# Converting eight instead of sixteen stages' weights ahead of the first block, with a new order of work, in a fused attention and two-layer network kernel

## The chip, the core and the metric

The kernel runs on one core of a Trainium2 chip. The core has a matrix engine (TensorE, PE in the profile, with its weight loads shown as PEld), a vector engine (VectorE, DVE), an activation engine (ScalarE, ACT), a general engine (GpSimd, POOL) and a queue for transfers (SyncE, SP). ACT can issue transfers too; all transfers run on the same sixteen DMA engines. The metric is device time in microseconds (us) of one run of the whole program.

## What is computed

The reference chains three parts. B = 2 batches, H = 8 heads, S = 768 positions, D = 64.

```python
q_assign = np.argmax(np.einsum('bhsd,hcd->bhsc', q_n, c_n), axis=-1)   # 16 centroids per head
k_assign = np.argmax(np.einsum('bhsd,hcd->bhsc', k_n, c_n), axis=-1)
mask = q_assign[:, :, :, None] == k_assign[:, :, None, :]
scores = np.where(mask, scale * np.matmul(q, k.transpose(0, 1, 3, 2)), -1e9)
attn = softmax(scores); x = np.matmul(attn, v)          # 1536 tokens x 512

h = x @ w_in                                            # 512 x 2048
g = np.where(h >= 1, h, np.where(h <= -1, 0.0, (h + 1) ** 2 / 4))
x = g @ w_out                                           # 2048 x 512

h = (x @ w1) * (x @ w2) @ w3                            # 512 x 1024, 1024 x 1024
out = h @ w_out2                                        # 1024 x 512
```

All five weight matrices come as 64-bit floats.

## The kernel before

**Blocks and stages.** A block is one batch of 768 tokens. Attention of a block is cut into units of two heads (a *pair*, 0 to 3 in block 0) and these into tiles of 128 queries by 768 keys, 48 tiles a block, numbered 0 to 95. For each tile PE makes the scores (`s`, L859), DVE their row maximum (`smax`, L867), GpSimd scales it (`sbias`, L872), ACT takes the exponential (`sexp`, L880), and PE transposes the result (`spT`, L897), which ACT or DVE copies out (`sT`, L352 or L354); in block 1 most tiles are split in two 16-bit halves and transposed by a DMA instead. When six tiles are there, PE multiplies them with v (`pv`, L968 and L976). Before the scores of block 0 stand the centroid products (`am`, L539, which need k or q of two pairs), some ten DVE instructions of the form L555 to L590 that turn them into masks, and small triangular matmuls (`ah`, L580).

Behind attention, block 0 passes through *stages* of the two networks, in the order of a list `seq`: `h` and `y` stages for the first (16 of each, L1239), then 16 `ab` stages and 8 `o` stages. Each stage needs a weight chunk of 128 x 512. The product of w3 and w_out2 (`wp`, L1169) is made beside the attention of block 0. Block 1 goes through the same stages later, most of them by a scheme with seven products instead of eight (L1492).

**A weight chunk** is made in `chunk`. A chunk that still has 64-bit words is loaded (512 KB, L1101, issued by ACT), converted to 32 bits by two ACT instructions (`wabs` L1107, `wr` L1111) and two DVE instructions (`wc`, L1115 and L1121), and, if it is used again, stored as 256 KB into the DRAM tensor `wd` (SP, L1126). For use it is split into a high half (`whi`, ACT or DVE) and a low half (`wlo`, GpSimd or DVE, L357), since PE makes three passes over split operands. A chunk that lies in `wd` already is only loaded (256 KB, L1103, by ACT) and split. The first stages of `seq` are converted ahead, beside the attention of block 0, one between every few steps of `wp`:

```python
ahead = [weights_of(st) for st in seq[:AHEAD]]
ahead_n = {n for n, _ in ahead}
...
while ahead and len(ahead) * 2 * KF2 > AHEAD * (2 * KF2 - 1 - n):
    x, src = ahead.pop(0)
    chunk(t + dt / 2, src, True, False, keep=x)
...
return chunk(t, wd[n], False, needs=[("wd", n)]) if blk or n in ahead_n else chunk(t, src, True, keep=n)
```

With `AHEAD = 16` these are the stages h 0 to 5, y (0, 0 to 3), h 6 to 9 and y (1, 0 to 1); all later ones are converted in the stage itself ("in place").

**The order.** Nothing schedules at run time. A table of characters, `ORDER`, lists all 3036 steps of the kernel and for each the engine that does it where there is a choice; the steps are emitted in this order, so each engine has its instructions in the order in which they stand there. Waits between engines are set where one step reads or overwrites what another made. Transfers share eight completion semaphores in turn, so a transfer that takes one up again waits until the transfer that had it before has landed. PE also has 40 filler steps (`idle_mm`, L469, two matmuls each as the profile counts them) that multiply an identity and feed nothing; score tile 6 comes behind all of them.

**The first loads.** SP loads k and q of the four pairs of block 0 (`kq0`, L513, 384 KB each, eight loads) and then v of pair 0 (L736). ACT issues the first four chunks of w_out2 (L1101, shown as in_w_out_dram) and the first of w3. ACT's first work is to round q and k to the format of PE (`qh`, `kh`, `k2h`, `q1h`, all L352; `qh1.0` is the rounding of q of pair 1, head 0), DVE's and GpSimd's to make the remainders (`qlo`, `klo`, L357).

Of the kernel before, what the change touches and what calls it, by code (L numbers as in the profile page):

```python
# [43 lines left out]
    ",4,(,*,,,6<6<F<J&9<L<N<8<:<<&E&I<?+m+|,#,.&K,8,:,<<s,%<V,0,2,><g&>%%<@,@,L=*=:<e,B,D+g,N,P,F,R,X,Z,],_<i<k<Z"
    "<n<]<p,e,g<`<a;|<0<2,H,T,a,J<u+i+l,u,w=J<w=X<y<|+o=#%@&@&B<B<Q<R,V,c,y,|=,=<=i=>-(&P=.-#-*+r-,-.-4-6-%-8-:=0"
    "<q=%&c-0-2=@+s=2=4=6=B=D=(%>=y=N-<-@&U-B-D=L=Z=]-L,i,l=P=R=U=V&L-X-Z-]-N-P>0=_,m,o-F->=k>@=a=m=o=d=e=q=s>#-_"
    "=|>P-R-H-u-K-w-y>%>(>4>2>6-e-g=8=F,r-a.(.*.,>D-T-V&_-c&i>a-|>8,s=g=u>+&l&o&e&[=H>-.4.6.8=w>:&W&^&R&b&n>B>F>H"
    ".#-i-m>K&X>L&u..>o.%.0-k.@.B.3.D-o?#>.>=>>%*>e&s.L.N>R>T>V>c&g?4.:.X.<.Z>N>q>s-q.F>X>Z%B.P.R.T.>?(>g>u?%.]?F"
    "._>i.H.J.V>w?*>l>z>]?,?.?0>n>~.a.u.c?V/(/4/*/,&z&|/@-s.w/B/D(&?8?i?@&w>_?2?B?D/.(-($%,/6?6&q?J?H((%D.m.y.|/#"
    "?:?L(.?Z?X?]?<?N/8/:/<?>/%?_?k?m?o?a?Q?q?R/0/2/>%.%0%2.e.g?y%4?s?u/F%F/L/N%H%6/H%J?T?c?e@2@B/J/X%L%8@T@#/P/R"  # L50
    "/T@,?g%:%</Z.i.k?|@4@e0(0*@%.o@(@*/]/_/e/g/V.q?w@.@0/a/c.s@w@6/u/w(*@D0,0.@8@:@=/y@>%N040608@F@H@J@X/|/m@i@V"
    "@g@Z00%P0#0%%R@k@m@]@`@a@N@L@o%T@@@PA.0:020<0?0@0L0N0P0B0D@y@|/i/k/oA2A#A%A)A*0X@q@RA:@c@s@u0u0w0y0FA@0R0T/q"
    "0Z0]APAcA0A40H0J0W0|0_A,A<A>0e0gABADAF(0(2/sA6A8(4(61#0a0c1(1*0iAs1416ATARAVAX0lAZAH1,1.AeAgAiA]AkAKAM1%181:"
    "AwB%0m0o1012AmAo1X1Z1@1L1N1P1B1D1](:Au(=ANA_AaB,1<1R1T(8(AAy(>(BA|(MB#(N1_1FAqB(1H1>B*(D1e1g1J1V(FBJ(H1a1d0r"
    "1i2*(Z(J0s2,2.1u1k1w1y20B.B022(P1|(R24Bi1m1o1rC.BLBO1s2#2%26(TBkBmB2B4B6CL2((V(X282:2<B8B>B@Ck2>BBC12F2H2J2@"
    "2B2DBPBR2LBTBDB;2NB=BV2PBFBIB]B_BaBcBfC2C4C6FLC82T2V2XCNFe2c2eBXCQ2gC:Bg2RBZ2Z2^2_BoBqC<BsB|C#2i2kC?D0BuBxC&"
    "C(2m2a2oC@CBCD3%3(C+(]3*BzCRCTCn3,CoCWCFCH3436383/D>30D3C_CaCcCeC,CX3:3<D#3>2q323B2y3@CK(b3D(d(_(e3P3RCZD@D4"
    "D6D%DLD(3F3HD*3K3L3NCg(h3T3VDZ3XC^3ZD:CjD9CqCsCuCwDB2s3_D<3a3cDN3m3]D]3oCz(iDi3q3e3hDDDG3i3k(tD-E.3sG#(lDHDJ"
    "DPDR2u(nD_4>Da3u3wDk2w2|DTEL(pDn(uC~3#3y4042FP44463|Dc4@4B)(DVE1E2(w4D4GDeDg(q484:4H4JEkD/DYF0ENF>EP(yDoDqDs"
    "4L4N4<4PFiDuDxFND|E#4RFR4#EnFTEoE%E(4TGL4VDz4XFg4ZE4E6E*Fk4]4_E-FmFoE8E:4%4(E@EBF24aG(4*4,Gu4.FVF54c4e4gEEEF"  # L60
    "G%E<E?EI(|)#)%)*G*G,G.F#5:F%F(F*ERETEWEXEKHDE_5<5>F@F6F8FBEaE[E]GPEcEe5@Gy4i4k4m5B5D5FGNGRGT4oEqFYFZEsEuEwF:"
    "4q4s4uF-4w4y4|FqFsEyHmGwG|FHH#F<5H5JHHF/I,EhFJHFEjHJHLGVH%HNFDFFHq5#5,5.5LG05%5(FaFc5*G3E~F]FyF|HoHsHu5N5PHw"
    "F_FuGXGZH)IDI05V5X5R5T5ZH+I.FwI2I4I]G@GBGDGF5]5e5g5i5_5aGHGJ),G4G6).G9)1I65cIa)2G]G_5kHQGa5mHR)4G:G<5s50545u"
# [1694 lines left out]
```

## Time and profile before

| | us |
|---|---|
| median of 3 runs | 719.14 (718.37 to 720.06) |
| the profiled execution, its own time | 719.4 |
| its span, first to last instruction | 717.7 |
| PE / DVE / ACT / POOL busy | 697.5 / 615.3 / 467.4 / 279.6 |

The span is what the profile divides up; 1.7 us of the profiled execution's time lie around it. Matmuls are pipelined, so busy time of PE does not mean that PE is at its peak, but time in which PE is not busy is a wait of the whole chain when nothing else is left for PE to do. TensorE's granted clock is 0.998 of full speed over the span.

### The profile page before, as it was taken

To read this page: it belongs to the slowest core of one execution; us is meant where nothing else is said; L and a number is where in the kernel's file an instruction comes from. 1 tells how busy PE (TensorE), PEld (TensorE's weight loads), DVE (VectorE), ACT (ScalarE), POOL (GpSimd) and SP (SyncE) were. 2 spreads that over 40 slices of the span, in tenths; PEclk is the share of its full clock that TensorE was granted. 3 is DMA by queue.
4 is the path that set the end of the run, shared out by engine and by line. 5 is a ranking of instruction groups with operands and counts; after the bars stand their busy time and mean duration, and the time that the engine had idled before them with its cause. 6 is when DMAs were issued, how large, how long until landed. Compare 5 with 4: busy or idle time off the path is not lost.

```text
span 717.7 us, 12011 instructions
## 1 busy us (share of the span) xinstructions
PE 697.5 (97%) x4185; PEld 633.1 (88%) x4185; DVE 615.3 (86%) x1087; ACT 467.4 (65%) x873; POOL 279.6 (39%) x351
## 2 busy tenths in 40 slices
PE   4999999999999999999999999999999999999998
PEld 1967777677798989899989999999999999999997
DVE  6989999999989989999989998668888797999940
ACT  7889999878876677896786756324844444543211
POOL 2343424222334324344443332323644525387520
PEclk9999999999999999999999999999999999999999
DMA  8247866977989989798889987663133112122211
GB/s 323 85 147 232 296 212 217 293 246 232 229 187 194 227 204 228 193 222 222 232 213 239 227 224 186 136 196 120 45 103 88 46 59 73 59 61 74 87 63 56
DMA packets 122509, 121.58 MB, mean 169 GB/s; under 512 B 80656, under 2 KB 89296, under 8 KB 122448
## 3 DMA queue, kind: packets, MB, share of 16 engines
q1 hardware_dynamic: 99888, 61.39, 34.7%
q10 hardware_dynamic: 22560, 59.42, 26.6%
q8 instruction: 33, 0.54, 0.3%
q14 instruction: 28, 0.23, 0.1%
HBM read 75.79 MB, written 22.28 MB: 137 GB/s over the span
## 4 chain that ended last, share of the span: by engine, by line
PE 80%; ACT 5%; DVE 5%; issue 2%; DMA 1%; ACTq 0%; POOL 0%; SPq 0%; DVEq 0%; POOLq 0%
PE mo L1239 37%; PE sc L1492 9%; PE sc L859 7%; PE mo L1492 6%; PE sc L1239 5%; PE av L976 3%; PE mo L1169 3%; PE av L1239 3%; PE sc L897 2%; PE av L968 2%; PE av L1492 2%; ACT P L880 2%; DVE nm L867 1%; ACT pt L352 1%; DMA wf<-wp 1%
## 5 line engine op out<-in xcount | busy, mean ns | idle before, releaser
L1239 PE MATMUL mo<-X,whl 128*128 128x384 f32 x912 | 169.0, 338 | 0.8 <-DVE Yp L354 0.8
L1239 PEld LDWEIGHTS mo<-X,whl 128*128 128x128 f32 x912 | 158.5, 188 | 3.1 <-DVE Yp L354 1.2
L357 POOL TENSOR_TENSOR whl<-wf,whl 128x512 fp32r<-128x512 f32 x69 | 92.0, 1335 | 128.4 <-DVE whl L354 53.6
L1239 PE MATMUL mo<-G,whl 128*128 128x384 f32 x684 | 126.2, 339 | 0.0
L1239 PEld LDWEIGHTS mo<-G,whl 128*128 128x128 f32 x684 | 120.4, 188 | 0.8 <-ACT phl L352 0.3
L867 DVE TENSOR_REDUCE nm<-sc 128x1 f32<-128x768 f32 x96 | 89.7, 950 | 9.5 <-PE sc L859 6.9
L872 POOL TENSOR_SCALAR nm<-nm 128x1 f32<-128x1 f32 x96 | 30.1, 313 | 132.8 <-DVE nm L867 122.4
L352 ACT ACTIVATE whl<-wf 128x512 fp32r<-128x512 f32 x63 | 39.3, 628 | 36.8 <-PE mo L1239 19.0
L859 PE MATMUL sc<-k,q 128*128 128x512 f32 (+1 forms) x192 | 53.5, 359 | 1.9 <-ACT pt L352 1.2
L1107 ACT ACTIVATE wf<-w 128x512 f32<-128x512 f32 x72 | 48.0, 674 | 11.3 <-POOL whl L357 6.3
L1111 ACT ACTIVATE w<-w,down 128x512 uint32<-128x512 uint32 x72 | 54.6, 767 | 0.2
L880 ACT ACTIVATE P<-sc,nm 128x768 f32<-128x768 f32 x52 | 46.6, 900 | 11.3 <-POOL nm L872 6.6
L1121 DVE SCALAR_TENSOR_TENSOR wf<-w,wf 128x512 uint32<-128x512 uint32 x72 | 51.8, 726 | 1.2
L1115 DVE SCALAR_TENSOR_TENSOR wf<-wf,w 128x512 uint32<-128x512 uint32 x72 | 49.6, 695 | 1.0 <-ACT wf L1107 0.4
L859 PE MATMUL sc<-kq 80*128 80x512 f32 (+1 forms) x192 | 49.4, 339 | 0.0
L880 ACT ACTIVATE sc<-sc,nm 128x768 f32<-128x768 f32 x44 | 38.2, 869 | 15.9 <-POOL nm L872 15.4
L357 DVE TENSOR_TENSOR phl<-sc,phl 128x768 f16<-128x768 f32 x44 | 41.8, 951 | 6.6 <-ACT phl L352 5.9
L897 PEld LDWEIGHTS sc<-ident,P 128*128 128x128 f32 x312 | 35.0, 140 | 10.4 <-ACT P L880 6.8
L897 PE MATMUL sc<-ident,P 128*128 128x128 f32 x312 | 40.7, 275 | 2.4 <-ACT P L880 2.3
L352 ACT ACTIVATE pt<-sc 128x768 f32<-128x768 f32 (+1 forms) x46 | 36.4, 811 | 5.8 <-PE sc L897 4.7
L859 PEld LDWEIGHTS sc<-k,q 128*128 128x128 f32 x192 | 31.5, 189 | 9.0 <-ACT pt L352 3.7
L357 DVE TENSOR_TENSOR whl<-wf,whl 128x512 fp32r<-128x512 f32 x43 | 31.0, 721 | 9.2 <-ACT whl L352 8.7
(238 smaller groups left out, 1458.8 us busy)
## 6 DMA issues: line engine op xcount, KB each, us to landing
wf<-wd ACTq DMA_DIRECT2D x64, 256.0 KB, 2.7
w<-in_w_out_dram ACTq DMA_DIRECT2D x24, 512.0 KB, 4.6
wd<-wf SPq DMA_DIRECT2D x48, 256.0 KB, 3.4
w<-in_w3T_dram ACTq DMA_DIRECT2D x16, 512.0 KB, 4.6
...
```

The lines of the kernel that those rows point to most:

```text
L352: nc.scalar.activation(out=out, in_=in_, func=AF.Copy)
L357: (nc.gpsimd if e == "POOL" else nc.vector).tensor_tensor(out=out, in0=a, in1=b, op=ALU.subtract)
L859: nc.tensor.matmul(ps[:, n], q[0:n_rows, q0:q0 + 128], k[0:n_rows, n], start=first, stop=not first)
L867: nc.vector.tensor_reduce(out=nm, in_=T[("sc", b), s], axis=AX.X, op=ALU.max, negate=True)
L880: nc.scalar.activation(out=new(("P", b), s).rearrange("p n s -> p (n s)") if by_pe(s) else T[("sc", b), s], in_=T[("sc", b), s], func=AF.E ...
L897: nc.tensor.transpose(T[("sc", b), s][:, c], p[:, c], ident)
L1107: nc.scalar.activation(out=T["wf", i], in_=T[w64, i].bitcast(F32)[:, :, 1], func=AF.Abs, scale=float(2.0 ** -112))
L1111: nc.scalar.activation(out=lo, in_=lo, func=AF.Identity, scale=float(2.0 ** -29 - 2.0 ** -41), bias=down)
L1115: nc.vector.scalar_tensor_tensor(out=w, in0=w, scalar=3, in1=T[w64, i][:, :, 0], op0=ALU.logical_shift_left, op1=ALU.bitwise_or)
L1121: nc.vector.scalar_tensor_tensor(out=w, in0=T[w64, i][:, :, 1], scalar=0x80000000, in1=w, op0=ALU.bitwise_and, op1=ALU.bitwise_or)
L1239: nc.tensor.matmul(acc, w[:, a, k4 * 128:(k4 + 1) * 128], rhs(c, k4), start=(first and k4 == 0 and n == 0), stop=(last and k4 == 3 and n = ...
L1492: nc.tensor.matmul(ps, lhs(av, a, k), rhs(bv, c, k), start=k == 0 and n == 0, stop=k == 1 and n == 2,)
```

## The change

`AHEAD` becomes 8. The stages h 0 to 5 and y (0, 0 to 1) are still converted ahead; y (0, 2 to 3), h 6 to 9 and y (1, 0 to 1) are now converted in place. For each of these eight a load of 64-bit words and the four conversion steps move into its stage, the store into `wd` (for block 1) with them, and the load from `wd` in block 0 falls away: 3028 steps instead of 3036. `ORDER` is replaced by another table for these steps, so that also steps that have nothing to do with weights stand elsewhere or on another engine.

```diff
@@ -36,63 +36,63 @@
 ORDER = (
-    "###%#*#,#0#.$.$V%X#(%V%[#2$0#4%e%h%c%q$6$8$:$<$>$X$_$a$c$e%b%k$2$4$H%]:m:|%y&,%_%i;0;>$@$B$D%m;L$]$Z$q#B$g$i"
+    "###%#:#<#*#,#0#.#($0$V%X%[$.#2#4$Z$]$X$4%e%h%]%V%b%c%q%y&,$6$8$:$<%|#8#Z%_:m:|$_$a%m%k;0$q#N$>$@$c$e$D$2$H$s"
...
 )
@@ -372,7 +372,7 @@
     LATE = 8.0
     W_AFTER = []
     V_AHEAD = 4
-    AHEAD = 16
+    AHEAD = 8
     U_DVE = 4
     N_IDLE, N_IDLE1 = 40, 0
     W_SIDE = 1
```

**SP at the start.** These are the first loads of k and q (in_kT_dram, in_qT_dram) and of v in SP's queue, before:

```order
L513 DMA kq_119<-in_kT_dram 128x768
L513 DMA kq_119<-in_qT_dram 128x768
L513 DMA kq_119<-in_kT_dram 128x768
L513 DMA kq_119<-in_qT_dram 128x768
L513 DMA kq_119<-in_kT_dram 128x768 x2
L513 DMA kq_119<-in_qT_dram 128x768 x2
L736 DMA raw_93<-in_vT_dram 128x768
```

And with the change:

```order
L513 DMA kq_119<-in_kT_dram 128x768
L513 DMA kq_119<-in_qT_dram 128x768
L513 DMA kq_119<-in_kT_dram 128x768
L513 DMA kq_119<-in_qT_dram 128x768 x3
L513 DMA kq_119<-in_kT_dram 128x768 x2
L736 DMA raw_93<-in_vT_dram 128x768
```

The pairs, which the rows do not name, were k0 q0 k1 q1 k2 k3 q3 q2 and are now k1 q0 k0 q2 q3 q1 k3 k2: the last load was q of pair 2 and is now k of pair 2.

**ACT at the start.** These are ACT's rounding of k and q (L352; kq_105 and kq_106 belong to pair 0, k_101, kq_107 and q_104 to head 0 of pair 1) and its first weight loads (L1101, w), before:

```order
L352 ACTIVATE kq_105<-kq_119 64x768
L352 ACTIVATE k_99<-kq_119 64x768
L352 ACTIVATE kq_106<-kq_119 64x768
L352 ACTIVATE k_100<-kq_119 64x768
L352 ACTIVATE kq_106<-kq_119 64x768
L352 ACTIVATE kq_105<-kq_119 64x768
L1101 DMA w_113<-in_w_out_dram 128x1024
L1101 DMA w_114<-in_w_out_dram 128x1024
L352 ACTIVATE k_101<-kq_119 64x768
L352 ACTIVATE q_102<-kq_119 64x768
L352 ACTIVATE kq_106<-kq_119 64x768
L1101 DMA w_115<-in_w_out_dram 128x1024
```

And with the change:

```order
L352 ACTIVATE kq_105<-kq_119 64x768
L352 ACTIVATE kq_106<-kq_119 64x768
L352 ACTIVATE kq_105<-kq_119 64x768
L352 ACTIVATE k_99<-kq_119 64x768
L352 ACTIVATE k_100<-kq_119 64x768
L352 ACTIVATE k_101<-kq_119 64x768
L352 ACTIVATE kq_107<-kq_119 64x768
L352 ACTIVATE q_102<-kq_119 64x768
L1101 DMA w_113<-in_w_out_dram 128x1024
L1101 DMA w_114<-in_w_out_dram 128x1024
L352 ACTIVATE q_103<-kq_119 64x768
L352 ACTIVATE kq_106<-kq_119 64x768
```

The first weight load now stands behind the rounding of k and q of pair 1 (k_101, kq_107); before it stood behind that of pair 0 alone.

**ACT in the first stages of block 0's network.** These rows stand beside the first y stages (Yp is their sum) and the attention tiles of block 1 (sc, phl, L880); wf<-wd is the load of a chunk that was converted ahead. Before:

```order
L352 ACTIVATE k_100<-raw_94 64x768
L1103 DMA wf<-wd 128x512
L880 ACTIVATE sc_1912,su<-sc_1912,nm 128x768
L1103 DMA wf<-wd 128x512
L880 ACTIVATE sc_1913,su<-sc_1913,nm 128x768
L1101 DMA w_115<-in_w_in_dram 128x1024
L352 ACTIVATE Yp<-mo_1907 128x384
L352 ACTIVATE phl_112<-sc_1913 128x768
L352 ACTIVATE whl<-wf 128x512
```

And with the change, beside the h stages just ahead of them:

```order
L880 ACTIVATE sc_1865,su<-sc_1865,nm 128x768
L1101 DMA w_113<-in_w_in_dram 128x1024
L1111 ACTIVATE w_114<-w_114,down 128x512
L1107 ACTIVATE wf<-w_114 128x512
L880 ACTIVATE sc_1866,su<-sc_1866,nm 128x768
L352 ACTIVATE phl_111<-sc_1866 128x768
L352 ACTIVATE phl_112<-sc_1865 128x768
L352 ACTIVATE whl<-wf 128x512
L1111 ACTIVATE w_115<-w_115,down 128x512
```

The 256 KB loads from wd have gone; 512 KB loads of 64-bit words and the two conversion steps L1111 and L1107 stand there.

## Rows read from the trace of the kernel before

**Rows 1.** The page, busy time and share of the span by engine.
```profile
PE 697.5 (97%) x4185; PEld 633.1 (88%) x4185; DVE 615.3 (86%) x1087; ACT 467.4 (65%) x873; POOL 279.6 (39%) x351
```

**Rows 2.** Windows by stage, whole span: each engine's busy us, PE clock, DMA share.
```profile
core 0: us, PE busy (x) PEld busy (x) DVE busy (x) ACT busy (x) POOL busy (x), PEclk, DMA share, GB/s
0.00:18.00 18.00, 7.45 (x37) 1.98 (x38) 10.99 (x29) 13.69 (x19) 5.31 (x14) 1.00 0.89 323
18.00:38.00 20.00, 19.91 (x141) 18.71 (x140) 18.18 (x29) 17.16 (x29) 6.27 (x9) 0.91 0.31 102
38.00:100.00 62.00, 60.68 (x368) 45.65 (x367) 57.59 (x96) 57.15 (x102) 25.41 (x34) 1.00 0.68 219
100.00:160.00 60.00, 57.83 (x348) 40.69 (x347) 57.29 (x87) 52.49 (x89) 19.63 (x25) 1.00 0.77 249
160.00:250.00 90.00, 88.84 (x537) 77.25 (x536) 81.76 (x130) 68.68 (x127) 29.07 (x44) 1.00 0.89 215
250.00:300.00 50.00, 48.52 (x293) 45.52 (x292) 45.27 (x75) 37.04 (x67) 16.80 (x23) 1.00 0.85 207
300.00:450.00 150.00, 150.00 (x951) 141.06 (x950) 138.01 (x221) 109.33 (x198) 58.32 (x70) 1.00 0.90 220
450.00:717.70 267.70, 264.25 (x1524) 262.26 (x1522) 206.26 (x425) 111.88 (x248) 118.75 (x135) 1.00 0.28 84
```

**Rows 3.** Timeline of PE to 22 us: start, us, operation, [idle before, releaser].
```profile
16.82 0.85 PE L539 MATMUL sc<-kq,cT 128*32 128x384 f32 x8 [2.52 <-DMA kq<-in_qT_dram]
```

**Rows 4.** Timeline of ACT to 22 us, its weight loads: issue time and us to issue.
```profile
5.54 0.39 ACTq L1101 DMA_DIRECT2D w<-in_w_out_dram  x1
...
8.13 0.35 ACTq L1101 DMA_DIRECT2D w<-in_w_out_dram  x1
...
10.08 0.33 ACTq L1101 DMA_DIRECT2D w<-in_w_out_dram  x1
```

**Rows 5.** Windows as in rows 2, of single stretches.
```profile
0.00:24.10 24.10, 13.55 (x74) 7.98 (x75) 16.14 (x38) 17.81 (x25) 7.12 (x15) 0.93 0.71 258
6.00:8.00 2.00, 0.33 (x2) 0.18 (x2) 1.32 (x4) 1.99 (x4) 0.00 (x0) 1.00 0.90 283
10.00:12.00 2.00, 1.65 (x9) 0.55 (x10) 1.90 (x4) 1.98 (x3) 1.42 (x2) 1.00 1.04 421
400.00:420.00 20.00, 20.00 (x130) 18.77 (x127) 18.53 (x30) 11.37 (x22) 6.90 (x9) 1.00 1.00 239
```

**Rows 6.** Timeline of DVE, 18 to 25 us, first and last row.
```profile
18.30 0.58 DVE L555 STREAM_TRANSPOSE P<-sc 128x384 f32<-128x384 f32 x1 [2.09 <-PE sc L580]
...
24.14 0.96 DVE L867 TENSOR_REDUCE nm<-sc 128x1 f32<-128x768 f32 x1 [0.54 <-PE sc L859]
```

**Rows 7.** Timeline of PE, 40 to 42 us: the first product with v.
```profile
41.16 1.19 PE L968 MATMUL av<-pt,vn 128*64 128x384 f32 x6
```

**Rows 8.** Waits of PE: us in total, times, longest.
```profile
PE sc L897 <- ACT P L880: 2.3, 4, 1.1
...
PE sc L859 <- ACT pt L352: 1.2, 5, 0.3
```

**Rows 9.** Groups by line: busy us, mean ns of one | idle before.
```profile
L357 POOL TENSOR_TENSOR whl<-wf,whl 128x512 fp32r<-128x512 f32 x69 | 92.0, 1335 | 128.4 <-DVE whl L354 53.6 <-ACT whl L352 47.6 <-issue 17.4
...
L1111 ACT ACTIVATE w<-w,down 128x512 uint32<-128x512 uint32 x72 | 54.6, 767 | 0.2
...
L1121 DVE SCALAR_TENSOR_TENSOR wf<-w,wf 128x512 uint32<-128x512 uint32 x72 | 51.8, 726 | 1.2
L1115 DVE SCALAR_TENSOR_TENSOR wf<-wf,w 128x512 uint32<-128x512 uint32 x72 | 49.6, 695 | 1.0 <-ACT wf L1107 0.4 <-ACT w L1111 0.2
L1107 ACT ACTIVATE wf<-w 128x512 f32<-128x512 f32 x72 | 48.0, 674 | 11.3 <-POOL whl L357 6.3 <-issue 2.7 <-DVE whl L357 1.1
...
L357 DVE TENSOR_TENSOR whl<-wf,whl 128x512 fp32r<-128x512 f32 x43 | 31.0, 721 | 9.2 <-ACT whl L352 8.7
```

**Rows 10.** The page, DMA queues: packets, MB, share of sixteen engines' span.
```profile
q10 hardware_dynamic: 22560, 59.42, 26.6%
```

More of the change, by code (lines that the diff above doesn't have):

```diff
@@ L44 @@
[L44 to L63, printed above, removed]
@@ new lines @@
+    "&<;s<*+L+@+N+P&%+2+>+B<H*i*k+X+Z<<&><:<>*o<@&9<B;u;x*r&G*s&7;Z+R+D+F+T+H+]<V+_+u+a+J+V+c+w+y;y,(,4,6&:<Z,*,,"
+    "<J;j<,+|&5%@+e<L&I<.+m;k<N<P<S<0<3<k,8,:,.,#,%<4,0,<,2,>,@,L,N,P,B,D&D<|&N,R=2,F,X,Z<U;|<$<%,u,w,T+g+i+l+o<X"
+    "<m<o,H,J<]<q<_&P,y,],|,_,W<s=#=%=(%(<6<E,a,c<a<d=@<u<w&@-(-*=6=4=T&B-,-.-#-4&c-6-8-&+r&M+s=*-:,e=8,g<e<g<i=,"
+    "<F%>-0-2&k&R=D=e-<-@-B=:-D-F-L-X-N-Z-]-P&K-?=u&T&W&Z=B=F=H=K-R===>=L&a,i,k,m,o&_&X&o>0-u-T-H-K-w-y-_>>-W,r<y"
+    "=/=0=V.(.*.,=g=w&]%B=X=i=Z,s=]=k-e-|=m=o-g-a&e-c=y=|=`&n>#=b=N=P=R>&>).4.#.6.8-i-k-m-o-r>L>B>]..&r&j&u>o.%&s"
@@ new lines @@
+    "-s.0.@.B>4=c=r=s%%%*>2>6.:&g>P>@>N.2.<.>>s>D.L.N>8>a.X.Z>*.D.F>R>T>;>W>=>F.P.R.T.H?,>_>Y.]>I._>K.u.J.a.V.c?<"
+    "/4/(>,>.&y&|&w/@>q>c>e>g>i.w(./6/8(%.y(#?0?@/*/,.|(-%,/:/.()%D>u/B/D>w>Z>k>m>z.e.m?.?2>~?>?B/#?D?%/</0/%/2/>"
+    "%.%0?4%2%4?N%F(*/F/L/N?e%H?6?8%6/H/J?#/P/R?P/X?F?(?*?H%J%L%8%:%<?u/T/Z.g.i.k?R.o0(0*.r.s?T?V?:?J?L/]/_/a/e/V"
+    "@./c?g?i0,@D?y?w?X/u@T/g/w/y%N?[04/m06?|0./|%P?k00?_080:?m@2@0%R@g@#?p?q@%@(@40#0%?]?a?c@6%T020<0>0@0L0B0D0N"
+    "0P/i0X0Z0]@9/k/o?s@;@*@,@F0u0w/r/s0y0R0F0T@H@X@J@k0H0K0_@>@L(4@<@@@B0|@V@Z@]0V@O@P0a0c(01((21*1,0e0g141#1618"
@@ new lines @@
+    "@i@mA#0m1.101%12@o@r@t@_@a1X1Z0i0k0oABA%1]A(1@1L1B1D1:CD1N(6(:(81F0q(=@w(>@R@c@e1<(A(C(M1_(N1H1J1P1R1e1gAa1>"
+    "(D@u@y@|AD(F1T0s1W1a1iAF1c2*2,B%(H1u1w(P1l2.202224BD1m1o1r1s1y1|Bc2#Ac2%(Z(R(T(V(J26(XCHAeC]A*28A,2:2(2<A.A0"
+    "A6B)B+2F2H2>A82@2BA;A2A4A<C(A?2JAHAJALAN2LAPAR2NB,B.CaB0A@2T2V2XATAV2Z2P(]2DBGB2BH2c2e2gAXB4B6C6CFAZA]Cu2^2_"
+    "AgAiAkAmA_2R2i2kCJApCLAsAu2aBeB8B:C*AwC,2m2oCNArBhB<3%3(3*AyC_B>CcCeBACgBJDDA~B#Cy3,3.BLBN3436Bi30BPCwC|D#38"
+    "3:3<BBBVBXB[DmDH3BE<C93DC:B]3>323@BuBwByCQB|BkDFBmDJBoCSB_DLDNBb3F3H3J3L(b(d2yC#(_(eDoBR3PC.3R3TC%C23ND%EeE@"
@@ L96 @@
+    "fVg8fJgsgwhqf]gufZgDgFg3h*h8fcgqgyf_fag:g<h.hVg|fefggHgJhXh#h2g>gNh&gRh(gLh0h4h6h,h<h>hDhbgUhshvgVh]hZg@h|hw"
+    "h:hdhHh@i$i%hJhLhehFgPhBgXi(gZg]hNhPhRhki4i7i9i>iPiZhyi<i.i0i+i2i,iAhniSi:iUiBiJiViDiLi]iXiGiHhoiNi`iaidiehh"
+    "hiigiiik"
 )
```

74 lines of the change are left out of this document (38 added, 36 removed).

## The prediction

> **What bounds the kernel now.** I read the page first: TensorE (PE) is busy 97% of the span, VectorE (DVE) 86% [rows 1]. Then the windows by stage [rows 2], which say where PE's missing time lies: 10.6 us idle before 18 us, 3.5 us between 38 and 160, 2.6 us between 160 and 300, nothing from 300 to 450, and 3.5 us behind the last matmul. The number of matmuls does not change, so the change can only move this idle time, about 16.7 us ahead of the tail. From 38 to 160 DVE runs beside PE at 94% (57.59 + 57.29 of 122 us): whoever wants PE earlier there must get DVE earlier too.
>
> Next the start, instruction by instruction. PE waits 2.52 us for a load of q and starts the last group of centroid products only at 16.82 [rows 3]. The reason is in the ACT queue's issues [rows 4]: ACT issues the first 512 KB weight load at 5.54, when two of the eight k and q loads (384 KB each) have landed. The later weight loads stand behind landings of k and q loads, because the eight completion semaphores go round: the issues at 8.13 and 10.08 follow the third and the fifth k or q load, so those came 0.98 us apart, (10.08 - 8.13) / 2. The last three then took from 10.1 to 16.7, 2.2 us each, because weights came in between. The DMA engines moved 283 GB/s at 6 to 8 us and 421 at 10 to 12 [rows 5]: the start is bound by loads, and what matters is which bytes come first. DVE waits with them: its transposition starts at 18.30 after 2.09 us idle, and the first row maximum of the softmax at 24.14 [rows 6]. The first product with v starts at 41.16 [rows 7]; from 18 us to there PE has no idle time worth the name, but part of its work is filler, the matmuls of `idle_mm`.
>
> Third, the waits of PE by releaser [rows 8]: 2.3 us on ACT's exponential and 1.2 us on ACT's copy of transposed scores, 3.5 us in all, the largest sort behind the start.
>
> **The change, part by part.** The new order leaves out eight loads of 256 KB from `wd`. It moves eight conversions from beside the attention of block 0 into the stages of block 0's network, where their weights are needed. And it is another table, so three things move that the words of the change do not say: the order of the first loads, which engine does what, and the order of PE's work.
>
> *The start.* The new SP order asks for q of pairs 2 and 3 before k of pair 3 and k of pair 2; the new ACT order puts its first weight load behind `qh1.0`, which waits for q of pair 1, the sixth load. So six loads run without weights beside them. At 0.98 us each from the second landing (5.5 us) the sixth lands at 9.4; if the third comes as late as now (8.1) it is 11.0; I take 10.2. The last two share with weights at 2.2 us each: 14.6, against 16.7 now. Behind the last landing stand now 0.85 us of products [rows 3] and, up to the first maximum, 7.3 us in all (24.14 - 16.82), with one more wait for PE inside. In the new order the last load is k of pair 2; behind it come 0.85 us of products and ten DVE instructions of about 0.56 us, the transposition's 0.58 [rows 6] being of their kind, 6.7 us with the hops. The first maximum then starts at about 21.4, 2.7 us earlier. The ends: if only DVE's own queue counted (the same instructions stand ahead of that maximum in both orders, 16.1 us of work in 24.1 [rows 5], so 8.0 us are idle, and about 3.8 of these lie before the first loads matter) it is 4.2 us earlier; if the order of the loads did not matter, 0.5 us. Of the 40 filler matmul pairs 18 instead of 13 now stand ahead of the first score tile, so PE has about 1 us less to do from there to the first product with v and does not hold the gain back. **Taken: -2.8** (-4.2 to -0.5).
>
> *DVE beside the attention of block 0.* Up to the maximum of tile 37 of the 48 the two orders have 201 DVE instructions each: the eight missing conversion halves (mean of 0.73 and 0.70, so 5.7 us) are filled with four low halves of weights that GpSimd had (0.72 instead of 1.34 on GpSimd) [rows 9] and with 13 others, while 9 others go. At a low half's price for these, +2.9 + 2.9 - 5.7 = +0.1. All of the swapped kinds lie between 0.4 and 1.0 us, so the sum can be off by 1.5. DVE is thus not relieved until tile 37, only later (246 against 241 instructions up to tile 47). The gain of the start survives on DVE but does not grow there. **Taken: 0** (-1 to +1.5).
>
> *ACT beside the attention of block 0.* Up to tile 47 seven fewer first halves (0.67) and eight fewer low-word conversions (0.77) stand in ACT's queue [rows 9], 10.9 us; 261 instructions become 239. PE waits 3.5 us for ACT [rows 8]. An exponential that is late because DVE's maximum was late is not helped, so I do not take all of it. **Taken: -1.2** (-3.5 to 0).
>
> *The moved conversions.* Each costs 1.44 us on ACT and 1.43 on DVE [rows 9], as before, now between about 160 and 250 us. ACT has 21 us free there, DVE 8 [rows 2]; eight conversions bring 11.5 and 11.4, but DVE loses other work up to the same tiles, so it is no fuller. The work that hides them is PE's own h and y stages; in ACT's queue each load stands nine to fourteen instructions ahead of the first half of its conversion. If that cover fails, a late weight stops PE, and everything queued on PE behind it, for the length of one conversion chain, some 3 us. The stages from 300 to 450 all convert in place already, with PE idle 0.00 [rows 2]. **Taken: +0.5** (0 to +4, below).
>
> *The left-out loads* were issued by ACT far ahead and nobody waits for them at length: 0.
>
> The sum is made against the profiled execution's own 719.4 us (717.7 of span and 1.7 around it): -2.8 + 0 - 1.2 + 0.5 = -3.5, so 715.9. That execution lies 0.3 above the median of 719.14, so **715.6 us** for the median.
>
> **The DMA engines, for and against.** A moved stage asks for 512 KB in and 256 KB out instead of 256 KB in: +4.2 MB for eight. At the price of queue 10, 59.42 MB in 26.6% of 717.7 us [rows 10], 3.2 us per MB, that is 13.5 us of all sixteen engines, into a stretch of 90 us with a share of 0.89 [rows 2], where 9.9 us are free. By occupancy 3.6 us do not fit.
> The Trainium skill (Perfetto Trace Analysis, Identifying the Most-Contended Engine) says that for DMA one should not go by occupancy, since sixteen engines make it misleading, but by the use of HBM. By that rule 215 GB/s [rows 2] beside the 421 of the start [rows 5] is half full, nothing overflows, and the term is 0 instead of 0.5: 715.1. This trace sides with it in one place: at 400 to 420 the share reads 1.00 and PE is not idle at all [rows 5].
>
> **The rivals.**
> 1. *More than forecast:* ACT's relief removes all 3.5 us of waits and the start gains its 4.2: 719.4 - 4.2 - 3.5 = 711.7 at the end, 712 to 714.2 as a case. For it: both orders' engines have the same work ahead of the first maximum. Against: DVE at 94% from 38 to 160.
> 2. *The start's gain is spent:* the new order has waits of its own. The old one shows 6.1 us of PE idle time between 38 and 300; half as much again would take 3 us back, and a share of the DVE sum at its upper end 1.5: 717.7 to 720.5.
> 3. *Slower:* the loads do not fit. Place: 160 to 250 us, ACT's weight loads and SP's transposes of scores on the same sixteen engines. If the share cannot rise above 0.89, the whole 13.5 us come late; half of it hidden by the early issue leaves about 7: 715.6 - 0.5 + 7 = 722. It decides from about 5 us more of PE idle time between 160 and 300 than the 2.6 there are. For it: the share is already 0.85 to 0.90 from 160 on, and score transposes run there. Against: the reading of 1.00 without an idle PE.
>
> **How the numbers follow.** Chances: the forecast (714.2 to 717.7) 0.47, rival 1 0.21, rival 2 0.19, rival 3 0.13. A change of 0.2%, 1.4 us, is about the least that these measurements tell from none. Faster than that (below 717.7) are the forecast and rival 1 with a little of rival 2: 0.70; within it most of rival 2: 0.17; slower 0.13. The range leaves out the lower edge of rival 1 and all of rival 3: 712.8 to 719.9. The forecast alone spans 714.2 to 717.7.
>
> **What would show it.** In the start: PE's wait for a q or k load below 1 us; first maximum at 21.4 +- 0.7; first product with v at 38.3 +- 0.9. Beside attention: waits of PE on ACT's exponential and copy below 2.5 us together. From 160 to 250: a DMA share of 0.95 or more with at most 2 us of PE idle; 56 instead of 64 loads from `wd`. From 450 on the same 3.5 us. The forecast is wrong if the first product with v starts later than 40, or if PE's idle time between 38 and 300 is above 8 us.

## The result, and the profile after

The changed kernel is slower: 725.70 us median of five runs (723.58 to 729.64) against 719.08 of five of the kernel before, ratio 1.0093 [1.0072, 1.0113]. The forecast of 715.6 (712.8 to 719.9) was wrong, and on the wrong side. The profiled execution is the fastest of the five, 723.58 with a span of 721.9, so its rows show the loss at its smallest. The same stages and columns as in [rows 2], after:

```profile
0.00:18.00 18.00, 10.96 (x70) 6.22 (x71) 13.62 (x34) 15.18 (x21) 7.41 (x15) 1.00 0.86 312
18.00:38.00 20.00, 18.26 (x128) 15.76 (x126) 18.13 (x33) 18.56 (x33) 5.70 (x9) 1.00 0.39 130
38.00:100.00 62.00, 61.56 (x374) 45.55 (x374) 59.44 (x94) 55.27 (x95) 22.63 (x32) 1.00 0.59 191
100.00:160.00 60.00, 59.30 (x354) 43.26 (x351) 56.24 (x87) 49.62 (x87) 13.79 (x23) 1.00 0.69 222
160.00:250.00 90.00, 83.86 (x499) 73.25 (x498) 73.59 (x114) 68.18 (x126) 32.39 (x44) 0.98 0.88 196
250.00:300.00 50.00, 49.31 (x318) 45.79 (x318) 46.16 (x77) 38.89 (x72) 23.64 (x30) 1.00 0.83 217
300.00:450.00 150.00, 149.02 (x922) 139.20 (x919) 134.55 (x220) 111.35 (x198) 63.74 (x72) 1.00 0.90 224
450.00:721.90 271.90, 267.36 (x1536) 264.05 (x1534) 208.83 (x429) 113.75 (x250) 115.67 (x133) 1.00 0.29 88
```

PE's idle time by stage, before and after: up to 38 us 10.6 and 8.8, from 38 to 160 3.5 and 1.1, from 160 to 300 2.6 and 6.8, from 300 to 450 0.0 and 1.0, from 450 on 3.5 and 4.5. All that was forecast for the first 160 us came, and more; then one stage gave it all back.

**Where the gain was.** The start, by the answers to [rows 3, 4, 6, 7], from the timelines of PE, ACT, DVE and PE:

```profile
13.35 0.85 PE L539 MATMUL sc<-kq,cT 128*32 128x384 f32 x8
```
```profile
10.63 0.87 ACTq L1101 DMA_DIRECT2D w<-in_w_out_dram  x2
```
```profile
20.36 0.95 DVE L867 TENSOR_REDUCE nm<-sc 128x1 f32<-128x768 f32 x1
```
```profile
38.20 1.19 PE L968 MATMUL av<-pt,vn 128*64 128x384 f32 x6
```

The first weight load is issued at 10.63 instead of 5.54, the last group of centroid products no longer waits for a load, and the first maximum comes 3.8 us earlier. The lead grows: the last products with v of block 0 start at

```profile
181.89 4.09 PE L968 MATMUL av<-pt,vn 128*64 128x384 f32 x24
```

in the timeline of PE, and before the change at

```profile
188.36 4.09 PE L968 MATMUL av<-pt,vn 128*64 128x384 f32 x24
```

that is 6.5 us earlier. Up to these two points PE has done the same 1050 matmuls; it was idle 15.3 us before and 10.5 after, and busy 173.1 and 171.4. So 4.8 us of the lead are waits, and 1.7 us are TensorE's clock: before the change, after the wait of 2.52 us for q, the granted clock was 0.91 in the mean of 18 to 38 us [rows 2] (0.50 from 19 to 21 us, the lower level of 1.2 GHz), and it is 1.00 now. At the end the changed kernel is 4.2 us later (721.9 - 717.7), so 10.7 us are lost behind that place.

**Where the loss is.** The waits of PE, against [rows 8]:

```profile
PE sc L859 <- DVE phl L357: 4.0, 1, 4.0
...
PE sc L859 <- ACT pt L352: 1.7, 6, 0.6
...
PE sc L859 <- DMA kq<-mask: 1.3, 1, 1.3
...
PE sc L897 <- ACT P L880: 0.5, 2, 0.3
```

The 4.0 us and the 1.3 us are single waits, both of the first score tiles of block 1, both between 190 and 205 us. No wait of PE for a weight is among them. Windows of 5 us there:

```profile
185.00:190.00 5.00, 4.75 (x32) 3.83 (x27) 3.77 (x7) 4.52 (x9) 1.51 (x3) 1.00 0.99 228
190.00:195.00 5.00, 3.67 (x21) 3.19 (x20) 3.86 (x6) 1.91 (x4) 1.41 (x2) 1.00 1.26 138
195.00:200.00 5.00, 3.55 (x21) 3.23 (x19) 0.37 (x1) 0.00 (x0) 0.00 (x0) 1.00 1.15 115
200.00:205.00 5.00, 2.46 (x8) 2.28 (x9) 3.02 (x5) 3.79 (x8) 1.41 (x3) 0.73 1.13 219
205.00:210.00 5.00, 5.00 (x29) 4.91 (x27) 3.87 (x7) 5.00 (x11) 4.13 (x6) 0.93 0.77 145
```

From 195 to 200 us DVE, ACT and POOL do next to nothing, while the DMA engines are over-full by their share (1.15) and move only 115 GB/s. The same stretch before the change, in which the second of the two transposes named below runs:

```profile
195.00:200.00 5.00, 5.00 (x31) 4.82 (x30) 4.32 (x6) 3.10 (x6) 1.53 (x3) 1.00 0.98 144
```

A low rate at a full share is there too, and PE is never idle: the sign by itself says little. After PE has stood still (from 198.5 to 202.5 us) its mean granted clock is 0.73 and then 0.93 for 5 us each, so part of that time it ran at the lower level, 1.2 GHz instead of 2.4; that is at most (0.27 + 0.07) x 5 = 1.7 us more. The queue of SP and then ACT show who waits for what:

```profile
183.50 0.33 SPq L513 DMA_DIRECT2D raw<-in_kT_dram  x1
183.92 0.47 SPq L721 DMA_DIRECT2D kq<-k  x1
184.44 0.59 SPq L722 DMA_DIRECT2D q<-kq  x1
185.08 0.59 SPq L724 DMA_DIRECT2D kq<-mask  x1
186.31 1.90 SPq L927 DMA_TRANSPOSE pt<-phl  x1
189.89 7.36 SPq L778 DMA_TRANSPOSE vn<-phl  x1
```
```profile
187.15 0.34 ACTq L1101 DMA_DIRECT2D w<-in_w_out_dram  x1
...
192.12 0.57 ACT L1247 ACTIVATE tmp<-mo,half 128x384 f32<-128x384 f32 x1
200.69 0.81 ACT L352 ACTIVATE phl<-sc 128x768 f16<-128x768 f32 x1 [7.99 <-DMA pt<-phl]
```

Two transposes by DMA, of tile 49's scores and of unit 4's v, hold the two buffers `phl` of block 1, which take what is to be transposed as 16-bit halves. Between their issues ACT issues a 512 KB load: chunk 41, one of the moved conversions. From issue to landing (DMA issues of 186 to 201 us):

```profile
w<-in_w_out_dram ACTq DMA_DIRECT2D x1, 512.0 KB, 13.3
...
pt<-phl SPq DMA_TRANSPOSE x1, 14.3
vn<-phl SPq DMA_TRANSPOSE x1, 13.3
```

Before the change the same two transposes, issued at 192.42 and 196.57, had no 512 KB load beside them (DMA issues of 192 to 202 us):

```profile
pt<-phl SPq DMA_TRANSPOSE x1, 5.3
vn<-phl SPq DMA_TRANSPOSE x1, 5.3
```

In the changed kernel ACT needs a free `phl` for tile 50's high half and stands still for 7.99 us, with all of its queue behind it; DVE's low half waits for ACT, and PE's scores of tile 52 need the score buffer that this low half frees.

### The profile page after: what moved, and what is told of

Same layout as the page of the kernel before. It is cut to its first block, busy times and chain, and to the rows that moved or that the text cites. A ratio compares the mean times of both kernels' runs of the same rounds, so it can differ in the third digit from the quotient of the medians.

```text
span 721.9 us, 11971 instructions
## 1 busy us (share of the span) xinstructions
PE 699.6 (97%) x4185; PEld 633.1 (88%) x4185; DVE 610.6 (85%) x1081; ACT 470.8 (65%) x874; POOL 285.0 (39%) x356
## 4 chain that ended last, share of the span: by engine, by line
PE 77%; DVE 11%; ACT 4%; DMA 3%; issue 2%; POOL 1%; SPq 0%; ACTq 0%; DVEq 0%; POOLq 0%
PE mo L1239 34%; PE sc L859 8%; PE sc L1239 6%; PE mo L1169 6%; PE sc L1492 5%; PE sc L897 4%; PE mo L1492 4%; PE av L976 3%; PE av L968 3%; DMA pt<-phl 2%; PE av L1239 2%; DVE tv L1403 2%; ACT pt L352 1%; PE av L1492 1%; DMA kq<-in_qT_dram 1%
## 5 line engine op out<-in xcount | busy, mean ns | idle before, releaser
L357 POOL TENSOR_TENSOR whl<-wf,whl 128x512 fp32r<-128x512 f32 x59 | 79.9, 1353 | 115.5 <-ACT whl L352 60.4
L1239 PE MATMUL mo<-G,whl 128*128 128x384 f32 x648 | 120.5, 340 | 0.0
L1239 PEld LDWEIGHTS mo<-G,whl 128*128 128x128 f32 x648 | 113.7, 188 | 0.9 <-DVE X L357 0.2
L352 ACT ACTIVATE whl<-wf 128x512 fp32r<-128x512 f32 x73 | 45.7, 628 | 49.3 <-PE mo L1239 16.2
L859 PE MATMUL sc<-k,q 128*128 128x512 f32 (+1 forms) x192 | 53.7, 361 | 7.0 <-DVE phl L357 4.0
L1111 ACT ACTIVATE w<-w,down 128x512 uint32<-128x512 uint32 x72 | 54.2, 764 | 1.1 <-issue 1.0
L1115 DVE SCALAR_TENSOR_TENSOR wf<-wf,w 128x512 uint32<-128x512 uint32 x72 | 52.3, 731 | 1.0 <-ACT wf L1107 0.7
L880 ACT ACTIVATE P<-sc,nm 128x768 f32<-128x768 f32 x52 | 46.4, 896 | 8.5 <-DVE P L555 2.8
L859 PE MATMUL sc<-kq 80*128 80x512 f32 (+1 forms) x192 | 49.9, 341 | 1.3 <-DMA kq<-mask 1.3
L1121 DVE SCALAR_TENSOR_TENSOR wf<-w,wf 128x512 uint32<-128x512 uint32 x72 | 50.0, 696 | 1.1
L1107 ACT ACTIVATE wf<-w 128x512 f32<-128x512 f32 x72 | 47.4, 668 | 4.7 <-DMA wd<-wf 2.2
L880 ACT ACTIVATE sc<-sc,nm 128x768 f32<-128x768 f32 x44 | 38.2, 867 | 14.8 <-POOL nm L872 14.4
L1239 PE MATMUL sc<-G,whl 128*128 128x384 f32 x252 | 46.2, 339 | 0.0
L357 POOL TENSOR_TENSOR G<-tmp,G 128x384 fp32r<-128x384 f32 x28 | 31.0, 1112 | 35.6 <-ACT G L352 21.6
L1239 PEld LDWEIGHTS sc<-G,whl 128*128 128x128 f32 x252 | 44.6, 188 | 0.1
L859 PEld LDWEIGHTS sc<-k,q 128*128 128x128 f32 x192 | 31.7, 190 | 14.4 <-DVE phl L357 5.1
L352 ACT ACTIVATE pt<-sc 128x768 f32<-128x768 f32 (+1 forms) x44 | 34.4, 811 | 13.5 <-PE sc L897 13.2
```

The lines of the kernel that those rows point to most:

```text
L352: nc.scalar.activation(out=out, in_=in_, func=AF.Copy)
L357: (nc.gpsimd if e == "POOL" else nc.vector).tensor_tensor(out=out, in0=a, in1=b, op=ALU.subtract)
L859: nc.tensor.matmul(ps[:, n], q[0:n_rows, q0:q0 + 128], k[0:n_rows, n], start=first, stop=not first)
L880: nc.scalar.activation(out=new(("P", b), s).rearrange("p n s -> p (n s)") if by_pe(s) else T[("sc", b), s], in_=T[("sc", b), s], func=AF.E ...
L1107: nc.scalar.activation(out=T["wf", i], in_=T[w64, i].bitcast(F32)[:, :, 1], func=AF.Abs, scale=float(2.0 ** -112))
L1111: nc.scalar.activation(out=lo, in_=lo, func=AF.Identity, scale=float(2.0 ** -29 - 2.0 ** -41), bias=down)
```

## The experiments

All times are medians beside runs of the kernel before on the same chip (719.0 to 719.7 us in the five comparisons). Unless said otherwise the ratio is to those.

**Chunk 41's load later, e1.** In the changed kernel the load and the step that first reads it move down ACT's queue:

```diff
 L762 ACTIVATE phl_112<-raw_93,vsc 128x768
 L1111 ACTIVATE w_113<-w_113,down 128x512
-L1101 DMA w_114<-in_w_out_dram 128x1024
...
 L352 ACTIVATE phl_112<-sc_1866 128x768
+L1101 DMA w_114<-in_w_out_dram 128x1024
```

> The changed kernel, with one 512 KB weight load (chunk 41) and the step that first reads it put behind tile 51's scores on ScalarE's queue; nothing else moves. Theory A (one collision: the first DMA transposes of block 1 meet this load): tile 49's transpose lands within 7 us of its issue instead of 14.3, ScalarE's idle stretch of 8 us at 192 to 200 us falls below 3 us, the granted clock stays at 1.00 there, and the time falls by 4 to 8 us, to 717 to 721. Theory B (what slows the transpose is all that is outstanding when it is issued, the q, k and mask loads of SP above all): the transpose still takes over 10 us and the time stays within 2 us of 725.7. Theory C (the loss is spread, from 4.2 MB more of loads and twelve more conversions before 300 us): within 2 us of 725.7 too, with the lag coming back somewhere behind.

Measured: 716.76 us (716.06 to 717.98), ratio 0.9965 [0.9952, 0.9978]. One load's place is worth 8.9 us. A window and DMA issues (188 to 194.3 us, then 198 to 199) of its profile:

```profile
190.00:200.00 10.00, 10.00 (x58) 9.57 (x57) 8.11 (x12) 8.10 (x16) 3.56 (x5) 1.00 1.08 222
```
```profile
pt<-phl SPq DMA_TRANSPOSE x1, 6.3
vn<-phl SPq DMA_TRANSPOSE x1, 5.6
```
```profile
w<-in_w_out_dram ACTq DMA_DIRECT2D x1, 512.0 KB, 3.9
```

PE is busy all the time. Tile 49's transpose takes 6.3 us instead of 14.3 and the load 3.9 instead of 13.3, although it is issued at 198.60, between two later transposes of scores, at 196.64 and 201.18, which land in 4.5 and 4.0 us: a load from ACT's queue and transposes from SP's can be in flight together at no such cost. The time is a little below theory A's range; B and C fall as they stood on record.

**SP's k load later, e2.** In the changed kernel, on SP's queue:

```diff
-L513 DMA raw_94<-in_kT_dram 128x768
 L721 DMA kq_106<-k_100 64x768
...
 L778 DMA_TRANSPOSE vn<-phl_112 128x12x128
+L513 DMA raw_94<-in_kT_dram 128x768
```

> The changed kernel, with SP's load of the next unit's k (raw, 512 KB, issued at 183.5 us ahead of the transpose) put behind the two transposes on SP's queue; the weight load of chunk 41 stays. Theory A: the transpose still stands beside the weight load and takes over 10 us, the time stays within 2 us of 725.7. Theory B: the transposes find 512 KB less ahead of them, land 3 us and more earlier, and the time falls by 3 to 7 us, to 719 to 723. Theory C: within 2 us of 725.7.

Measured: 719.13 us (716.06 to 723.51), ratio 0.9999 [0.998, 1.0017]. (The load is 384 KB; the text on record gives it as 512.) That speaks for B, and A falls as it stood: 6.6 us of the time are gone, though the runs scatter over 7 us. The load of chunk 41 is still issued by ACT 0.9 us behind tile 49's transpose. DMA issues of 187.4 to 195 us:

```profile
w<-in_w_out_dram ACTq DMA_DIRECT2D x1, 512.0 KB, 6.5
...
pt<-phl SPq DMA_TRANSPOSE x1, 7.6
vn<-phl SPq DMA_TRANSPOSE x1, 5.2
```

So both loads belong to it; neither is the cause alone.

**The load put into the kernel before, e3 and e7.** On ACT's queue of the kernel before, one load (e3) or two (e7), taken from their places at 205 us (not shown):

```diff
 L762 ACTIVATE phl_112<-raw_93,vsc 128x768
+L1101 DMA w_113<-in_w_out_dram 128x1024
+L1101 DMA w_114<-in_w_out_dram 128x1024
 L352 ACTIVATE whl<-wf 128x512
```

> The kernel before, with one 512 KB weight load (chunk 56, at 205.20 us) put where the changed kernel has one: on ScalarE's queue right behind the shift of unit 4's v, about 1 us behind the issue of tile 49's transpose. No byte is added. Theory A: the transpose takes 10 us and more instead of 5.3, ScalarE waits for its buffer, and the time rises by 4 to 8 us, to 723 to 727. Theory B: what stood outstanding ahead of the transpose is as before, so it takes at most 7 us and the time stays within 1.5 us of 719.1. Theory C: no change, within 1.5 us.

> The kernel before, with two of its own 512 KB weight loads (chunks 56 and 57, at 205 us) put on ScalarE's queue right behind the shift of unit 4's v, so that 1 MB stands beside the two transposes of block 1's first scores, where one load alone cost nothing. No byte is added. Theory A: the loads and the transposes overlap for more than 5 us, one of the two transposes takes 9 us or more, ScalarE waits for a score buffer, and the time rises by 2 to 7 us, to 721 to 726. Theory B' (it needs the changed kernel's pile of k, q and mask loads 2 to 3 us ahead of the transpose too): at most 1.5 us, within 718 to 721.

Measured: e3 719.38 us, ratio 1.0 [0.9986, 1.0014]: one load there costs nothing, against A as I had it. In its profile the load, 0.9 us behind tile 49's transpose and from the other queue, takes 5.5 us and the transpose 6.6. e7 723.97 us (722.18 to 727.23), ratio 1.0068 [1.0044, 1.0093]: two loads cost 4.6 us, in a kernel in which nothing else was changed. In e7's profile the transpose of v took 9.2 us, ACT's waits (186 to 212 us) and PE's timeline show the same chain as in the changed kernel, shorter:

```profile
ACT phl L352 <- DMA vn<-phl: 3.0, 1, 3.0
```
```profile
209.72 0.50 PE L859 MATMUL sc<-k,q 128*128 128x512 f32 x1 [1.91 <-DVE phl L357]
```

So a pile-up is enough to make the old kernel slow, and it takes more than one load.

**The same bytes, earlier, e6.** In the changed kernel, on ACT's queue:

```diff
 L352 ACTIVATE pt_96<-sc_188 128x768
+L1101 DMA w_114<-in_w_out_dram 128x1024
 L1103 DMA wf<-wd 128x512
...
 L1111 ACTIVATE w_113<-w_113,down 128x512
-L1101 DMA w_114<-in_w_out_dram 128x1024
```

> The changed kernel, with the 512 KB weight load of chunk 41 put ahead of chunk 35's load on ScalarE's queue, so some 5 us earlier and ahead of the k, q and mask loads of SP. Nothing else moves: the same bytes are outstanding when tile 49's transpose is issued or have landed shortly before. Theory A, now sharper (what costs is that the load and the transposes run on the DMA engines at the same time for long, and both then run at half their rate): the load is done before the transposes start, they land within 9 us of their issue, and the time is 716 to 719.5. Theory B (bytes outstanding around the transpose, in whatever order): the transpose still takes over 10 us and the time stays above 722.

Measured: 717.67 us (716.49 to 721.67), ratio 0.9979 [0.9965, 0.9993]. The load is issued 7 us earlier than in the changed kernel's profile and lands at 183.8, before SP issues its k load at 184.1. Earlier is as good as later: the loss needs this load in flight beside the transposes. Whether it needs the k load as well this run can't tell, since both are apart here; e2 says that it does.

**The same bytes at the same place, another queue, e15.** In the changed kernel SP issues the load, between the two transposes:

```diff
 L927 DMA_TRANSPOSE pt_97<-phl_111 128x12x128
+L1101 DMA w_114<-in_w_out_dram 128x1024
 L778 DMA_TRANSPOSE vn<-phl_112 128x12x128
```

> The changed kernel, with chunk 41's load issued by SP, the queue of the transposes, between the transpose of tile 49 and that of unit 4's v, instead of by ScalarE at about the same time. Same bytes, same place. If two queues that take turns on the DMA engines make both slow: tile 49's transpose lands within 8 us of its issue and v's within 9, ScalarE's idle stretch of 8 us goes below 4 us, and the time is 717 to 720. If it is the bytes beside the transposes, whatever the queue: the first transpose still takes over 10 us, and the time is 723 to 728.

Measured: 717.30 us (716.42 to 720.66), ratio 0.9981 [0.9966, 0.9995], 8.4 us less than the changed kernel. From its profile SP's queue, then the windows:

```profile
187.69 1.69 SPq L927 DMA_TRANSPOSE pt<-phl  x1
191.27 3.97 SPq L778 DMA_TRANSPOSE vn<-phl  x1
```
```profile
187.00:192.00 5.00, 4.75 (x31) 4.31 (x28) 3.93 (x6) 4.35 (x8) 1.29 (x1) 1.00 1.02 225
192.00:197.00 5.00, 4.06 (x23) 3.52 (x22) 3.87 (x7) 2.57 (x5) 1.41 (x2) 1.00 1.18 238
197.00:202.00 5.00, 5.00 (x30) 4.91 (x30) 3.74 (x6) 4.54 (x10) 3.20 (x4) 1.00 1.21 247
```

The DMA engines move 238 and 247 GB/s where they moved 138 and 115 in the changed kernel with the same transfers. The transpose of tile 49 lands after 8.1 us instead of 14.3 (just above the 8 that was named), that of v after 8.6 instead of 13.3, and ACT's wait for `phl` is 1.8 us instead of 8.0. So bytes alone are not the cause: with the k load ahead and the same bytes beside the transposes, the other queue helps. (The load also goes out 1.7 us behind tile 49's transpose instead of 0.8; this run doesn't part the two.) Two queues alone are not the cause either: in e2 and e3 load and transposes come from two queues too, 0.9 us apart, and the load takes 6.5 and 5.5 us, tile 49's transpose 7.6 and 6.6. The Trainium skill (DMA: Bandwidth & Descriptors, Queues, rings and completion order) says that each DMA engine takes turns between the queues that have work for it, a packet of descriptors at a time; e15 would fit it, but e2 and e3 show that such turns need not be dear, and why they are behind the k load no run here shows.

**The start alone, e4.** On ACT's queue of the kernel before:

```diff
 L352 ACTIVATE kq_105<-kq_119 64x768
-L1101 DMA w_113<-in_w_out_dram 128x1024
-L1101 DMA w_114<-in_w_out_dram 128x1024
 L352 ACTIVATE k_101<-kq_119 64x768
 L352 ACTIVATE q_102<-kq_119 64x768
 L352 ACTIVATE kq_106<-kq_119 64x768
+L1101 DMA w_113<-in_w_out_dram 128x1024
+L1101 DMA w_114<-in_w_out_dram 128x1024
```

> The kernel before, with the first four weight loads put behind three more of ScalarE's steps (behind the copy of unit 0's q), so that the q and k loads of the start have the DMA engines for themselves as in the changed kernel. Nothing else moves. If the start gain of the prediction is right (2.8 us, and still there at the end): TensorE's wait of 2.52 us on a q load before 16.82 us falls below 1 us, the first max comes 2 to 4 us earlier than 24.14, and the time falls to 715.5 to 717.5. If the gain at the start is spent on later waits: the first max comes earlier too, and the time stays between 718.4 and 719.8. If the four conversions behind the later loads take its place: above 719.8.

Measured: 716.64 us (714.88 to 717.81), ratio 0.9957 [0.9941, 0.9973]: 3.0 us, kept to the end. (Only two of the four loads change their place; the other two stood behind these steps already.) In its profile the last group of centroid products and the first maximum, in the timelines of PE and DVE, against [rows 3, 6]:

```profile
12.69 0.85 PE L539 MATMUL sc<-kq,cT 128*32 128x384 f32 x8
```
```profile
20.55 0.96 DVE L867 TENSOR_REDUCE nm<-sc 128x1 f32<-128x768 f32 x1
```

The start's gain is real, and it has nothing to do with how many stages are converted ahead: here all sixteen still are.

**The conversions' own price, e9.** The order of e1, with

```diff
+            if 40 <= i < 48:
+                low_floor = shift_low = sign = lambda e: None
```

> The changed kernel with chunk 41's load later, and three of the four conversion steps left out for the eight chunks 40 to 47 (one of ScalarE, two of VectorE each: 8 x 0.7 us and 16 x 0.6 us; their weights are then not the reference's); the loads and the step that writes the chunk stay. What goes is the engines' price of the moved conversions. Prediction's term (0.5 us, the engines have the time): 716 to 717.3, as with the later load alone. Rival (the conversions stand in the way of the scores' and the experts' steps on VectorE, 2 us and more): 713.5 to 715.

Measured: 718.97 us (716.91 to 721.88), ratio 0.9989 [0.9975, 1.0003]. The rival's 713.5 to 715 is out, and so is the 716 to 717.3 of the prediction's term. Windows of 160 to 250 us, where the moved conversions stand, first of e1, then of e9:

```profile
160.00:250.00 90.00, 89.17 (x536) 78.21 (x535) 80.48 (x126) 74.44 (x138) 34.69 (x48) 1.00 0.87 221
```
```profile
160.00:250.00 90.00, 89.19 (x537) 78.37 (x536) 71.25 (x111) 69.87 (x130) 34.77 (x48) 1.00 0.90 223
```

DVE has 9.2 us and ACT 4.6 us less to do, and PE's idle time is 0.8 us in both: in that stage of these two profiles the moved conversions cost PE nothing. But a kernel that does less than e1 is 2.2 us slower (1.7 by the two ratios), and I can't say why. Differences of 2 us between such orders are therefore not to be read as prices.

**The old order behind the changed beginning, e8, e10, e11, e12.** Each is e1 up to a step, and from there the kernel before's order and engines (the table alone changes):

> The changed kernel with chunk 41's load later, and from about 335 us on (tile 76's scores) the order and engines of the kernel before for everything still to come; the work is the same. In the profile with the later load alone 2.3 us of the gain were lost behind that place, 0.9 us at 350 to 370 us and 1.4 us at 640 to 655 us (two waits of TensorE on VectorE). If these are the new order's doing and not the conversions': both are gone and the time is 713.5 to 715.5. If what is lost there follows from the conversions or loads that were moved: 716 to 718 as with the later load alone.

> The changed kernel with chunk 41's load later, and the order and engines of the kernel before from about 410 us on (tile 87's scores), a place where the two orders have nearly the same steps behind them. Run e8 showed no wait of TensorE at 600 to 660 us with the old order, but lost 10 us at its own seam at 338 to 348 us, where VectorE was late. If the waits behind 450 us (0.5 us at about 508, 0.2 at 526, 1.2 at 645 to 655) are the new order's: they are gone, TensorE is busy for 60.0 of the 60 us from 600 on, and the time is 714 to 716. If the seam costs as in e8: above 718.

> The same with the old order from about 474 us on. If the waits behind 450 us are the new order's: 714 to 716, as with the seam at 410. If the seam costs: above 718.

> The same with the old order from about 609 us on, where the two orders differ by two steps only, so that no seam is to be seen. The 1.2 us at 645 to 655 us are gone, those at 508 and 526 stay: 715 to 716.5, if the waits are the new order's; 716.5 to 717.5 if they are not.

Measured: e8 721.51 us, ratio 1.0033 [1.0018, 1.0047]; e10 719.50, 1.0004 [0.9983, 1.0026]; e11 724.87, 1.0079 [1.0052, 1.0105]; e12 719.06, 0.9994 [0.9978, 1.001]. None of the four is faster than the kernel before. e10 and e11 come out where a costly seam was named (above 718), e8 and e12 in none of their ranges: each seam, the place where one order passes into the other, makes a wait of its own, in e11 one of 5.5 us of PE on ACT, and even at 609 us, where only two steps differ, one of 1.2 us on DVE. As a test of the waits at 640 to 660 us they are clear (in e1's profile these are 0.9 us, not the 1.2 and 1.4 of the texts on record). Windows of 600 to 660 us, first of the changed kernel, then of e8:

```profile
600.00:660.00 60.00, 59.25 (x337) 58.51 (x335) 53.78 (x111) 29.02 (x68) 36.17 (x45) 1.00 0.19 59
```
```profile
600.00:660.00 60.00, 60.00 (x343) 59.79 (x343) 54.69 (x113) 28.74 (x67) 35.83 (x43) 1.00 0.20 59
```

PE has no idle time there with the old order, nor in e10; each of the two has one wait of 0.2 to 0.3 us at 680 to 686 us. So most of the 1.1 us that the changed kernel loses behind 450 us, where no step of the change lies, is the new order's doing.

**The change in the old order, e13 and e14.** The order of the kernel before wherever both have a step, and `AHEAD = 8`; in e14 also the later loads of e4:

> Eight stages' weights converted ahead instead of sixteen, as in the changed kernel, with the order and engines of the kernel before for every step that both have: the eight conversions left out ahead of the block leave gaps, and the same eight stand where the reloads of chunks 48 to 55 stood, their loads some 30 to 60 steps ahead of them and behind the first two transposes of block 1. If the smaller number of conversions itself gains what the prediction gave it outside the start (1.2 us of waits on ScalarE less, 0.5 us more for the moved conversions): 718 to 719, the first max at 24.1 as before. If it does nothing: 719 to 720. If the loads behind 200 us cost by themselves (4.2 MB more, in the time of the transposes): above 721, with waits of TensorE between 200 and 330 us.

> The same, with the first four weight loads behind three more of ScalarE's steps as in e4. If the start's gain has nothing to do with the number of conversions, it is 3 us again: 715 to 717. If fewer conversions and later loads add up to the gain of the searched order by 170 us (6.5 us): 712 to 714.

Measured: 794.02 us, ratio 1.1035 [1.1019, 1.1052], and 787.80, 1.0953 [1.0925, 1.0982]. No theory had that size; above 721 was named for e13, but with waits between 200 and 330 us. The profile of e13 has waits of PE on ACT and DVE all over block 0, 18.9 us on ACT's exponential alone, with a mean clock of 0.955. It tells nothing about the change by itself, only that its steps don't fit into an order made for another set of steps. e14 is 6.2 us faster than e13.

## Why the prediction was wrong, step by step

- **The start, -2.8: right in kind, too small.** (Its own steps give 2.7 to 2.8.) The wait for a load is gone. The first maximum is at 20.36, not at 21.4 +- 0.7; the upper end, 4.2 us, was nearer to the 3.8 measured. The first product with v is at 38.20, as forecast (38.3). e4 has 3.0 us of it at the end of the kernel. That the wait also cost 1.7 us through the clock is no term of the sum.
- **ACT beside attention, -1.2: right in the main.** The waits on the exponential and on the copy fell from 3.5 to 2.2 us (0.5 + 1.7), below the 2.5 named. Another wait on the exponential, of 0.5 us and new, comes before 38 us (of L859); with it they are 2.7. With DVE's term, which can't be seen by itself, PE's idle time from 38 to 160 fell by 2.4 us.
- **The moved conversions, +0.5 (0 to +4): this step failed.** It priced the conversions by what they take from ACT and DVE and by what happens if a weight is late. Both were right: e9 finds no price for PE in that stage, and no weight is late. What it left out is what a load costs the other users of the DMA engines. Chunk 41's load, close behind SP's k load, met the two transposes that hold both `phl` buffers, and ACT, DVE and then PE waited for them; moving this one load, or issuing it from SP, gave back 8.0 to 8.9 us (e6, e15, e1).
- **The DMA engines, for and against** weighed bytes and share over 90 us. Both readings missed it: the share from 160 to 250 stayed at 0.88, not 0.95 and more, and 4.2 MB did fit once one load stood elsewhere. By the Trainium skill's rule (Perfetto Trace Analysis, Identifying the Most-Contended Engine) the term would have been 0, because 215 GB/s are half of the 421 at the start; at 115 GB/s, where ACT, DVE and POOL stood still behind a transfer, that measure is lower still. The measurement decides: here neither average saw the wait.
- **Rival 3 had the place, the price and the wrong mechanism.** It put 7 us between 160 and 250 us and decided from 5 us more of PE idle time between 160 and 300 than 2.6; there are 6.8, which is 4.2 more, and 1.7 us of lower clock. But it expected all loads to come late by occupancy. With a chance of 0.13 and a range that ended at 719.9 it was left out.
- **The signs of being wrong did not show.** The first product with v is not later than 40, and PE's idle time between 38 and 300 is 8.0 us (7.97), not above 8. The prediction was wrong all the same: what PE loses at the lower clock is no idle time, and these limits did not look behind 300 us.
- **From 450 on the same 3.5 us: wrong by 1.1** (3.45 and 4.54 us). Most of the waits vanish with the old order (e8, e10). The text argued only from what the change moves, and a new table is another order everywhere. Another 1.0 us between 300 and 450 was also not foreseen; its cause was not tested by itself.
- 56 loads from `wd` instead of 64: as said.

Left open: why runs of the changed kernel differ by 6 us (723.58 to 729.64) and those of e2 by 7 (an overlap of load and transposes that comes out differently each time would fit, and no run here shows it). Open too is what eight conversions ahead would be worth with an order that avoids the collision and the late waits. And open is why the transposes slow so much when chunk 41's load comes from ACT's queue close behind the k load, and so little without either of these. That the wait goes through the two `phl` buffers is read from the releasers in the traces; no run has a third buffer.
